# Packed attention with a convolved gate: half of batch 2's convolution on VectorE, and another order

## The chip, the cores and the metric

One core of one Trainium2 chip. The time is device microseconds of the whole kernel. It is the median of three runs: 284.44 us (283.52 to 285.25). The profile is of one more execution.

## The reference

For each of 8 batches, with S = 576 positions, 8 heads of 64 channels and 32 packed queries per head (everything in float32):

```python
p_packed = softmax(p @ k.T / 8) @ v              # 32 x 64 per head
x = softmax(q @ p_packed.T / 8) @ p_packed       # 576 x 64 per head, 576 x 512 over all heads
gate = sigmoid(sum(conv_w[k] * x_shifted(4 - k) for k in range(5)))   # causal, per channel
out = (gate * (x @ w_val)) @ w_out               # 512 x 512 weights
```

w_val, conv_w and w_out arrive as 64-bit floats; the kernel turns them into float32 itself.

## The kernel before, in words

Each batch is one chain of stages, and each stage is a Python generator that issues one or a few instructions per step. A written list, ORDER (line 52), names the stages by letter and batch (`x2` is one step of stage x for batch 2, `s3.2` two steps of stage s for batch 3); `run` (line 690) takes the steps in that order. InOrder (line 77) keeps every engine's instructions in the order in which they were issued, so ORDER is the program order of all engines. The stages, with the letters of the list:

- K, V, Q, P, L load k, v, q, p and the weights through SyncE's queue. `fetch` (line 188) makes each large load wait until the third load before it has landed (AT_ONCE = 3). v comes in two halves per batch; its tile vm has two buffers.
- W, C, O turn the words of the weights into float32 (ScalarE, VectorE, GpSimd); C also makes cwb, the taps spread over rows for the convolution on TensorE.
- k and q transpose on VectorE. a (line 375) is the first attention: scores on TensorE (tile s), maximum on VectorE (nb), exponential on ScalarE, which also accumulates the sums (sm); on VectorE the sums get 1e-9 added and are inverted; then the exponentials are turned (at, copied to a1t) and multiplied with v (pv), and ScalarE scales the product into ppd.
- p turns ppd. s (line 443) makes the second scores and exponentials. t (line 464) divides by their sums in two groups of heads, one behind the other: sums and reciprocals (rs) and a transpose (a, the tile a2) on VectorE, a product on GpSimd, and a split of a2 into a high and a low part (a2h, a2l).
- w multiplies the packed values with w_val (wp, split into wph and wpl).
- x (line 505) yields the gate's input. For a batch in WHOLE (0, 1 and 2) `convolved` (line 534) does the whole convolution on TensorE: GpSimd multiplies the packed values with the five taps (kx), and TensorE multiplies a2, shifted by 0 to 4 positions, with kx, in two halves of 288 positions; ScalarE takes tanh of each result (tile sig). For the other batches TensorE mixes once (tile x), ScalarE copies the result to xp, and stage g does the rest.
- g (line 576) is the convolution for the other batches: for each of four groups of 128 channels ScalarE multiplies with the first tap, VectorE adds the other four (scalar_tensor_tensor, each reading and writing sig), and ScalarE takes tanh. The four channel groups follow one another.
- v (line 597) multiplies a2 with the packed values (val), VectorE multiplies with the gate, ScalarE makes the high part gvh, GpSimd the low part gvl.
- o (line 643) multiplies with w_out (tile o), in chunks of 128 positions; the result goes through osb to memory. For the last batch the products of the first three channel groups are made ahead, and the ones with the fourth come last.

The tiles sig have four buffers, xp two (kx lies in one of them), PSUM's big tile three (lines 19 to 44).

Of the kernel before, what the change touches and what calls it, by code (L numbers as in the profile page):

```python
# [57 lines left out]
v0 t1 a3.2 P4 a3 w1 O0.2 Q2 O0 v0 w1.2 v0 q2 p2 O0.2 x1 a3 x1 O0 x1 a3.2 O0 t1 a3.2 x1 L0 t1 O0.2 V3 q2 a3 x1 P4 O0.2
v1 x1 O0 K4 v1 s2 O0 V4 a3 O0 k4 a3 O0 v1 K4 O0 k4 s2 K5 s2.2 v1 s2 o0 s2 o0 p3 k4 Q3 v1.3 t2 v1.2 K5 v1 Q3 v1.2 a4 q3
o0 t2 a4.2 s2 a4.2 w2 V4 o0 s2 v1 t2 o0 w2 k5 s2 p3 a4 x2 q3 o0 v1 o0 w2 t2 s3 t2 o0 P6 Q4 t2 a4 v1 t2 s3 P6 s3 t2  # L60
s3.2 t2 s3.2 k5 s3 o0.2 a4 s3 v1 x2.3 Q4 a4 K6 a4 k5 a4.2 x2 o0 q4 t2 a4 t3 x2 v2 q4 x2 t3 a5 t3 v2 t3 a4.2 o1 t3 o0
t3 k6 K6 a5 t3 V5 v2 a5.2 t3 x3 Q5 x3 a4 v2 a5 k6 x3.2 t3 k6 v2 o1 v2 p4 v2 x3.3 t3 V5 Q5 o1 g3 a5.2 g3 p4 a5 v2 g3 o1
g3 v2.2 o1 s4 g3 s4 v2 g3 o1 v2 g3 a5 q5 s4 V6 v2 K7 g3 a5 o1 s4 a5.2 s4 v2 s4 g3 a5 t4 o1 w3.2 g3 o1 s4.2 v2 a6 a5 g3
t4 v2 a6 q5 a6 w3 o1 t4 v3 s4 g3.2 a5 V6 a5 g3 o1 a6 t4 g3 t4 o1 a6 p5 t4 o1 g3 p5 v3 Q6 s5 o1 v3 a6 o1 g3.3 s5 t4 v3
s5.2 v3 Q7 g3 o2 v3 s5 t4 o2 v3 o2 s5 v3.2 g3.2 s5 t4 v3.2 g3 x4 g3 o2.2 x4 v3 x4 o2 x4 v3 x4 K7 t4 x4 k7 g4 o2 s5 t5
q6 v3.2 a6 x4 k7 a6 o2 g4 w4 t5 Q6 g4 w4 g4.2 a6 o2 g4.2 t5 w4 g4 V7 a6 t5 a6 s5 a6 t5 g4.2 t5 g4 v3 o2.2 v4 o2 a6 g4
o3 g4 v4 o3 v4 t5.2 v4 g4 v4 o3 g4 a6 v4.2 g4 v4.2 g4 q6 a6.2 g4.2 v4 g4.4 x5.2 p6 t5 x5 o3 p6 o3 s6 g4 v4 x5 o3.2 t5
s6 v4 s6 v4 o3 s6.2 o3 s6 x5.2 k7 g5 o3 x5 s6 v4 t6 g5 w5 o3 g5.2 w5 s6 o3 a7 g5 v4 g5 V7 w5 o3 a7 v5 g5.3 a7.2 s6 g5
v5 g5 o3 a7 t6 v5 v4 a7 v5 a7.2 q7 o4 o3 g5 a7 g5 t6 g5.2 a7.2 g5 a7 t6.2 g5 a7 o4 v5.2 Q7 a7.2 t6 a7 o4 g5 o4 t6 g5.2
v5.2 q7 p7 t6 p7 v5 o4 t6 v5 s7 g5 s7.3 o4 g5 v5 s7.2 o4 g5 x6.2 v5 x6.2 v5 x6 o4.2 t6 t7.2 g5 o4 v5 x6 g6 x6 v5 s7 g6  # L70
o4 g6 w6.2 g6.2 w6 g6 v5 t7 o5 g6 o5 g6 t7 o5 v6 s7 o4 g6.3 t7 o5 s7 t7.2 o5 g6.3 v6.3 g6.2 v6.2 o5.4 v6 g6.2 t7 v6 g6
v6.2 g6.3 o5.2 g6 x7 o5 v6.3 t7 x7 o5 g6 x7.2 v6.2 w7 t7 o5 x7 w7 v6 o6 w7 v7 x7 g7 o6 g7.6 o5 x7 v7 g7 o6.3 v7 g7.3
# [29 lines left out]
def packed_attention_gated_conv(  # L102
# [272 lines left out]
    def attn_pack(b):  # L375
# [6 lines left out]
        for g in range(G):  # L382
            nb = tile_of("nb1", [P, 1], F32, f"nb1_{b}_{g}")
            dve.tensor_reduce(nb, s1s[g], axis=AX.XY, op=ALU.max, negate=True)
            yield
            a1 = a1s[g] = tile_of("a1", [P, S], F32, f"a1_{b}_{g}")
            act.activation(
                a1.rearrange("a (c i m) -> a c i m", c=2, i=NP),
                in_turn(s1s[g]),
                AF.Exp,  # L390
                bias=nb,
                accum_out=sm[:, g : g + 1],
            )
# [68 lines left out]
            yield  # L462

    def weighted(b):
        rs = tile_of("rs2", [P, G, NBLK], F32, f"rs2_{b}")
        a2 = st["a2", b] = tile_of("a2", [P, G, S], F32, f"a2_{b}")
        ah = st["ah", b] = tile_of("a2h", [P, G, S], F32R, f"a2h_{b}")
        al = st["al", b] = tile_of("a2l", [P, G, S], F32R, f"a2l_{b}")
        for g in range(G):
            t3, r3 = st["t2", b][:, g], rs[:, g]  # L470
            dve.tensor_reduce(r3, t3, axis=AX.X, op=ALU.add)
            dve.reciprocal(r3, r3)
            yield
            t3 = t3[:, :, :NP]
            pool.tensor_tensor(
                t3, t3, r3.unsqueeze(2).broadcast_to([P, NBLK, NP]), op=ALU.mult
            )
            yield
            dve.transpose(a2[:, g], t3)
            yield  # L480
            act.copy(ah[:, g], a2[:, g])
            yield
            (pool if b in ON_POOL["al"] else dve).tensor_tensor(
                al[:, g], a2[:, g], ah[:, g].bitcast(F32), op=ALU.subtract
            )
            yield

# [46 lines left out]
    def convolved(b):  # L534

        kx = tile_of("xp", [P, 2, PAD + S], F32, f"kx_{b}")
        kx = kx.rearrange("a n m -> a (n m)")[:, : G * NT * D]
# [7 lines left out]
        yield
        sigs = []
        for c in range(NC):
            st["sig", b, c] = tile_of("sig", [P, S], F32, f"sig_{b}_{c}")
            sigs.append(st["sig", b, c])
        for half in range(2):  # L550
            a2 = st["a2", b]
            two = [big(f"x_{b}_{half}_{n}") for n in range(2)]
            for back in range(NT):
                skip = back if half == 0 else 0
                end = half * HS + HS - back
                for g in range(G):
                    for hl in range(4):
                        pe.matmul(
                            two[hl // 2][D * g : D * g + D, hl % 2, skip:HS],
                            kx[heads[hl], g, NT - 1 - back, :],  # L560
                            a2[heads[hl], g, end - HS + skip : end],
                            start=(back == 0),
                            stop=(back == NT - 1),
                        )
            yield
            for c in range(NC):
                act.activation(
                    sigs[c][:, half * HS : half * HS + HS],
                    two[c // 2][:, c % 2, :HS],
                    AF.Tanh,  # L570
                    scale=0.5,
                )
                if c % 2:
                    yield

    def gate(b):
        if b in WHOLE:
            return
        for c in range(NC):
            x = st["xp", b, c // 2][:, c % 2]  # L580
# [3 lines left out]
            for kk in range(1, NT):
                dve.scalar_tensor_tensor(
                    acc,
                    x[:, kk : kk + S],
                    cw[:, c, kk : kk + 1],
                    acc,
                    op0=ALU.mult,  # L590
                    op1=ALU.add,
                )
                yield
            act.activation(acc, acc, AF.Tanh, scale=0.5)
            yield
# [139 lines left out]
```

## Time and profile before

| | |
|---|---|
| median of three runs | 284.44 us |
| the profiled execution | 284.7 us |
| its span, first to last instruction | 282.9 us |
| TensorE matmul busy | 251.4 us (89%), 3603 instructions |
| TensorE weight loads busy | 186.8 us (66%) |
| VectorE busy | 237.2 us (84%), 313 instructions |
| ScalarE busy | 164.5 us (58%) |
| GpSimd busy | 129.4 us (46%) |
| granted TensorE clock, mean | 0.980 |

Busy shares are of the span. In the profile's lines PE is TensorE's matmul, PEld its weight load, DVE VectorE, ACT ScalarE, POOL GpSimd and SP SyncE's queue, which issues all transfers. Every instruction goes through the same helper, so all lines are L85, and groups are told apart by the tiles: out<-in. A matmul of 32-bit floats has two records. Matmuls of different parts of the array overlap, so that a group's busy time is more than the time for which it holds TensorE up; the chain of waits gives that time.

### The profile page before, as it was taken

How to read it: one execution, taken by the hardware profiler on the slowest of the kernel's cores; microseconds unless marked ns; L12 is line 12 of the kernel's file. 1: busy time of each engine (PE TensorE's matmuls, PEld its weight loads, DVE VectorE, ACT ScalarE, POOL GpSimd, SP SyncE). 2: the span in 40 equal slices, each digit the busy share in tenths (PEclk: the TensorE clock that was granted, in tenths of full speed). 3: DMA queues.
4: the chain of work that ended last, by engine and by line, in shares of the span. 5: the costliest groups of instructions: out<-in, count | busy, mean ns of one | idle time of the engine just before them, and what ended most of it. 6: DMA issues, size and time to landing. Idle time of an engine off the chain costs nothing.

```text
span 282.9 us, 8353 instructions
## 1 busy us (share of the span) xinstructions
PE 251.4 (89%) x3603; PEld 186.8 (66%) x3603; DVE 237.2 (84%) x313; ACT 164.5 (58%) x307; POOL 129.4 (46%) x118
## 2 busy tenths in 40 slices
PE   0366397999999999999999999999999899998984
PEld 0144254776786777786878687758876688687763
DVE  2978779799789997789999999999998989687720
ACT  6245564677934664864746765667747645743321
POOL 1633577667788572423466324243156423422220
PEclk9989879999999999999999999999999999999999
DMA  7999989599649758816552540116111112111014
GB/s 258 330 292 310 226 270 264 164 238 287 179 153 306 207 161 237 257 43 203 150 180 81 191 132 37 39 75 179 66 39 41 48 63 76 39 74 39 0 50 172
DMA packets 25858, 43.54 MB, mean 154 GB/s; under 512 B 5834, under 2 KB 11998, under 8 KB 25822
## 3 DMA queue, kind: packets, MB, share of 16 engines
q1 hardware_dynamic: 25822, 43.02, 49.5%
q8 instruction: 28, 0.46, 0.7%
q14 instruction: 8, 0.07, 0.1%
HBM read 33.57 MB, written 9.44 MB: 152 GB/s over the span
## 4 chain that ended last, share of the span: by engine, by line
PE 55%; DVE 23%; ACT 9%; DMA 5%; issue 3%; POOL 2%; SPq 2%; POOLq 1%; ACTq 0%; DVEq 0%
PE o L85 20%; DVE sig L85 16%; PE val L85 11%; PE s L85 7%; PE x L85 7%; PE pv L85 4%; DMA vm<-in_v_dram 3%; ACT sig L85 3%; PE at L85 3%; PE wp L85 2%; POOL t L85 2%; SPq L85 2%; DMA p<-in_p_dram 1%; ACT gvh L85 1%; ACT osb L85 1%
## 5 line engine op out<-in xcount | busy, mean ns | idle before, releaser
L85 DVE SCALAR_TENSOR_TENSOR sig<-xp,cw,sig 128x576 f32<-128x576 f32 x80 | 75.0, 937 | 6.1 <-ACT sig L85 4.6
L85 POOL TENSOR_TENSOR gvl<-sig,gvh 128x576 fp32r<-128x576 f32 x32 | 49.3, 1541 | 55.8 <-ACT gvh L85 55.8
L85 PE MATMUL o<-woh,gvh 128*128 128x512 f32 x144 | 59.1, 411 | 0.8 <-ACT osb L85 0.7
L85 PE MATMUL o<-woh,gvl 128*128 128x512 f32 x144 | 57.2, 398 | 1.2 <-POOL gvl L85 1.1
L85 PE MATMUL o<-wol,gvh 128*128 128x512 f32 x144 | 56.9, 395 | 0.0
L85 PE MATMUL val<-a2h,wph 128*128 128x288 f32 x128 | 39.1, 305 | 0.0
L85 PE MATMUL val<-a2h,wpl 128*128 128x288 f32 x128 | 38.0, 297 | 0.9 <-DVE wpl L85 0.9
L85 PE MATMUL val<-a2l,wph 128*128 128x288 f32 x128 | 37.6, 294 | 0.0
L85 POOL TENSOR_TENSOR t<-t,rs 128x576 f32<-128x576 f32 x16 | 20.0, 1252 | 34.7 <-DVE rs L85 34.7
L85 PEld LDWEIGHTS o<-woh,gvh 128*128 128x128 f32 x144 | 27.0, 188 | 12.6 <-ACT osb L85 2.7
L85 PEld LDWEIGHTS o<-woh,gvl 128*128 128x128 f32 x144 | 27.1, 188 | 8.8 <-POOL gvl L85 2.5
L85 ACT ACTIVATE osb<-o 128x512 f32<-128x512 f32 x34 | 20.4, 599 | 18.4 <-PE o L85 14.8
L85 ACT CAST gvh<-sig 128x576 fp32r<-128x576 f32 x32 | 21.5, 671 | 16.4 <-DVE sig L85 16.0
L85 PEld LDWEIGHTS o<-wol,gvh 128*128 128x128 f32 x144 | 27.1, 188 | 5.0
L85 DVE SCALAR_TENSOR_TENSOR sig<-sig,val 128x576 f32<-128x576 f32 x32 | 23.8, 743 | 7.8 <-ACT sig L85 3.6
L85 POOL TENSOR_TENSOR t<-t,mx 128x576 f32<-128x576 f32 x16 | 21.2, 1328 | 18.3 <-DVE mx L85 18.3
L85 PEld LDWEIGHTS val<-a2h,wph 128*128 128x128 f32 x128 | 24.0, 188 | 4.4 <-issue 1.8
L85 PE MATMUL s<-kT,pT 32*32 32x288 f32 x512 | 15.5, 461 | 11.7 <-DVE kT L85 11.7
L85 PEld LDWEIGHTS val<-a2h,wpl 128*128 128x128 f32 x128 | 24.0, 188 | 2.1 <-DVE wpl L85 1.2
L85 ACT ACTIVATE sig<-sig 128x576 f32<-128x576 f32 x20 | 13.7, 685 | 19.4 <-DVE sig L85 19.1
L85 PEld LDWEIGHTS val<-a2l,wph 128*128 128x128 f32 x128 | 24.1, 188 | 0.0
L85 PEld LDWEIGHTS pv<-vm,a1t 96*32 96x32 f32 x768 | 12.8, 117 | 15.1 <-ACT p L85 5.1
(81 smaller groups left out, 444.2 us busy)
## 6 DMA issues: line engine op xcount, KB each, us to landing
km<-in_k_dram SPq DMA_DIRECT2D x16, 576.0 KB, 5.3
vm<-in_v_dram SPq DMA_DIRECT2D x16, 576.0 KB, 6.1
qm<-in_q_dram SPq DMA_DIRECT2D x16, 576.0 KB, 6.1
out_dram<-osb SPq DMA_DIRECT2D x36, 256.0 KB, 2.0
wv_words<-in_moe_w_val_dram SPq DMA_DIRECT2D x4, 512.0 KB, 4.5
wo_words<-in_moe_w_out_dram SPq DMA_DIRECT2D x4, 512.0 KB, 5.6
p<-in_p_dram SPq DMA_DIRECT2D x16, 64.0 KB, 5.9
cw_words<-in_moe_conv_w_dram SPq DMA_DIRECT2D x1, 20.0 KB
```

The costliest lines, as they stand in the source:

```text
L85: made = getattr(self.engine, op)(*args, **kw)
```

## The change

Batch 2 leaves WHOLE and is alone in HALF: channel groups 0 and 1 are convolved on TensorE as before, groups 2 and 3 are mixed, copied to xp and convolved by stage g. Stage g now works on one channel group (`g10` is batch 2's third), so that the list can put the steps of several groups in any order. The second group of stage t is a stage of its own, u. The sums of the first attention go to a tile that is filled with 1e-9 at the start, and a reduction over two numbers takes the place of the scalar add. ORDER is another list from its second line on. Cut to its core:

```diff
-WHOLE = (0, 1, 2)
+WHOLE = (0, 1)
+
+HALF = (2,)
...
+    sums = const.tile([P, B, G, 2], F32, name="sums")
+    pool.memset(sums, 1e-9)
...
-                accum_out=sm[:, g : g + 1],
+                accum_out=sums[:, b, g, :1],
...
-        dve.tensor_scalar_add(sm, sm, 1e-9)
+        dve.tensor_reduce(sm, sums[:, b], axis=AX.X, op=ALU.add)
         dve.reciprocal(sm, sm)
...
+    def taps(b, kx, two, half, hls):
+
+        a2 = st["a2", b]
+        for back in range(NT):
+            skip = back if half == 0 else 0
+            end = half * HS + HS - back
+            for g in range(G):
+                for hl in hls:
+                    pe.matmul(
+                        two[hl // 2][D * g : D * g + D, hl % 2, skip:HS],
+                        kx[heads[hl], g, NT - 1 - back, :],
+                        a2[heads[hl], g, end - HS + skip : end],
+                        start=(back == 0),
+                        stop=(back == NT - 1),
+                    )
...
+    def half_and_half(b):
+
+        kx = factors(b)
+        pp = st["pp", b]
+        act.copy(pp, st["ppd", b][:, 2])
+        xp = st["xp", b, 1] = tile_of("xp", [P, 2, PAD + S], F32, f"xp_{b}_1")
+        pool.memset(xp[:, :, :PAD], 0.0)
+        yield
...
+            two = [big(f"x_{b}_{half}_{n}") for n in range(2)]
+            for g in range(G):
+                for hl in range(2, 4):
+                    pe.matmul(
+                        two[1][D * g : D * g + D, hl % 2, :HS],
+                        pp[heads[hl], g * D : g * D + D],
+                        a2[heads[hl], g, hc],
+                        start=True,
+                        stop=True,
+                    )
+            taps(b, kx, two, half, range(2))
+            yield
+            act.copy(xp[:, :, PAD + half * HS : PAD + half * HS + HS], two[1][:, :, :HS])
+            yield
...
-    def gate(b):
-        if b in WHOLE:
-            return
-        for c in range(NC):
+    def gate(n):
+        b, c = divmod(n, NC)
```

In the new list SyncE issues, after q of batch 0: v of batch 1 (first half), the first part of w_out, k of batch 2 (first half), p of batches 2 and 3, v of batch 1 (second half). Before, it was: the first part of w_out, k of batch 2 (first half), p, v of batch 1 (both halves). The steps around it and the last ones, old and new:

```diff
-V0 a0.2 W0 a1 W0 a0 W0 C0 a1 W0 a0 W0 Q0.2 a0 L0 p0 a1 K2 p0 q0.2 a1 P2 s0 a1 C0.2 s0 C0 O0 s0 O0 s0 V1 s0.2 a1 s0 O0
-a1 C0 t0 C0 | s0 C0 s0 a1 V1 t0 x0 P2 O0 t0.2 a1 t0.3 a1 k2 a1.2 w0 O0 t0 a1 w0 a1.2 x0 a1 t0 w0 O0 t0 O0 Q1 k2 K2 L0
...
-v7 o6 g7 v7 o6 g7 o6.2 g7 v7 g7 v7 g7.2 v7 g7 v7 o7 g7 v7 g7.4 o7 v7.2 g7 v7.2 o7 v7.2 o7.16 o6.3
+V0 a0.2 W0 C0 W0 C0 a1 a0 Q0 W0 Q0 V1 a0 L0 a1 a0 K2 a1 q0.2 C0 p0 P2 p0 a1 W0 s0 a1 W0 s0 O0.2 s0.2 C0 s0.3 a1.3 O0
+s0 t0 C0 s0 C0 | C0 u0 t0 a1.3 P2 a1 u0 x0 w0 O0 t0 V1 O0.2 a1 O0 a1.2 u0 w0 x0 t0 a1 u0 O0 x0 O0 p1 L0 k2 O0 k2 O0 x0
...
+v7 g30 o6 g30 g29 v7 g31 o6 v7.2 g29 v7 o6 v7.3 g30 o6 g30 v7 g31.2 v7 g31 v7 g31 v7 o7 v7 o6 o7 v7 o7.2 v7 o7.13 o6
+o7 o6 o7 o6
```

## Rows read from the trace of the kernel before

**Rows 1.** Windows of five stages: start:end, length, busy time per engine, PEclk, DMA.
```profile
0.00:40.00 40.00, 18.54 (x430) 11.43 (x434) 28.75 (x47) 20.45 (x40) 19.09 (x23) 0.87 0.94 278
40.00:100.00 60.00, 56.98 (x1184) 41.39 (x1174) 53.21 (x71) 37.56 (x79) 42.96 (x37) 1.00 0.78 230
100.00:130.00 30.00, 30.00 (x579) 22.60 (x578) 25.32 (x34) 19.09 (x41) 12.60 (x13) 1.00 0.60 178
130.00:230.00 100.00, 98.66 (x1166) 74.82 (x1165) 96.16 (x127) 65.11 (x114) 41.13 (x37) 1.00 0.31 98
230.00:270.00 40.00, 38.89 (x234) 31.02 (x233) 32.33 (x35) 19.72 (x32) 12.16 (x10) 1.00 0.12 47
```

**Rows 2.** Waits of PE from 39 us to the end: total, times, longest.
```profile
PE o L85 <- POOL gvl L85: 1.1, 2, 0.8
...
PE val L85 <- DVE wpl L85: 0.9, 1, 0.9
```

**Rows 3.** Chain that ended last, TensorE part: start, length, tile, matmuls.
```profile
105.35 2.61 PE x L85 x80
...
115.08 0.67 PE x L85 x16
```

**Rows 4.** Groups by line: count | busy, mean ns | idle before.
```profile
L85 DVE SCALAR_TENSOR_TENSOR sig<-xp,cw,sig 128x576 f32<-128x576 f32 x80 | 75.0, 937 | 6.1 <-ACT sig L85 4.6
...
L85 ACT ACTIVATE sig<-xp,cw 128x576 f32<-128x576 f32 x20 | 15.4, 769 | 0.3
...
L85 ACT ACTIVATE sig<-sig 128x576 f32<-128x576 f32 x20 | 13.7, 685 | 19.4 <-DVE sig L85 19.1
...
L85 ACT COPY xp<-x 128x576 f32<-128x576 f32 x20 | 12.2, 638 | 2.1 <-PE x L85 1.9
...
L85 ACT ACTIVATE sig<-x 128x288 f32<-128x288 f32 x24 | 8.0, 414 | 4.7 <-PE x L85 4.7
...
L85 ACT ACTIVATE ppd<-pv,sm 128x64 f32<-128x64 f32 (+1 forms) x32 | 9.6, 340 | 10.3 <-PE pv L85 8.1 <-issue 1.1 <-ACT sig L85 1.0
```

**Rows 5.** Tile sig: ns min/median/max of the convolution taps.
```profile
L85 DVE SCALAR_TENSOR_TENSOR sig<-xp,cw,sig x80: 719/818/2064, 120.9 to 267.1; 128x576 f32<-128x576 f32 x80
```

**Rows 6.** Tile sm: ns min/median/max of the two short VectorE operations.
```profile
L85 DVE TENSOR_SCALAR sm<-sm x8: 158/554/1572, 17.8 to 197.1; 128x2 f32<-128x2 f32 x8
...
L85 DVE RECIPROCAL sm<-sm x8: 165/165/167, 18.7 to 197.3; 128x2 f32<-128x2 f32 x8
```

**Rows 7.** Timeline of VectorE, two stretches: start, length, operation.
```profile
149.25 0.82 DVE L85 SCALAR_TENSOR_TENSOR sig<-xp,cw,sig 128x576 f32<-128x576 f32 x1
...
149.99 0.75 DVE L85 TENSOR_REDUCE mx<-t 128x18 f32<-128x576 f32 x1
...
157.82 4.43 DVE L85 SCALAR_TENSOR_TENSOR sig<-xp,cw,sig 128x576 f32<-128x576 f32 x4
...
237.74 3.38 DVE L85 SCALAR_TENSOR_TENSOR sig<-xp,cw,sig 128x576 f32<-128x576 f32 x4
```

**Rows 8.** Timeline of GpSimd beside the four taps at 157.82.
```profile
158.43 1.50 POOL L85 TENSOR_TENSOR gvl<-sig,gvh 128x576 fp32r<-128x576 f32 x1 [2.11 <-ACT gvh L85]
```

**Rows 9.** Timeline of all engines, 22 to 42 us.
```profile
22.11 0.35 SPq L85 DMA_DIRECT2D wo_words<-in_moe_w_out_dram  x1
...
25.86 1.41 SPq L85 DMA_DIRECT2D vm<-in_v_dram  x2
...
31.60 0.68 ACT L85 ACTIVATE t<-t 128x576 f32<-128x576 f32 x1 [1.89 <-POOL t L85]
...
34.41 0.78 ACT L85 COPY a1t<-at 96x768 f32<-96x768 f32 x1
...
35.90 1.51 PE L85 MATMUL pv<-vm,a1t 96*32 96x64 f32 x48 [4.92 <-DMA vm<-in_v_dram]
...
40.56 1.78 PE L85 MATMUL x<-a,kx 32*64 32x288 f32 x36
```

**Rows 10.** Tile vm up to 50 us: loads of v, issue to landing.
```profile
DMA to landing us min/median/max: 6.1/7.6/10.2
```

More of the change, by code (lines that the diff above doesn't have):

```diff
@@ L58 @@
[L58 to L72, printed above, removed]
@@ new lines @@
+a3.2 w1 a2.2 a3 v0 p2 w1 p2 O0 w1 u1 V3 q2 t1 v0 O0.2 x1.2 a3 x1 Q2 a3 P4 q2 a3 P4 O0 a3 O0 V3 x1 a3.2 L0 O0.3 u1 x1
+Q3 O0 v1 O0 x1 s2 O0.2 v1 K4 k4 v1 O0 s2 k4 v1 O0 v1.2 s2 v1 Q3 v1 s2 v1 o0 K4 a3 o0 k4 s2 a3 K5 s2 v1 a4 K5 s2 w2
+o0.2 s2 q3 v1 a4 p3 a4 s2 v1 V4 t2 a4 v1 a4 u2 t2 q3 w2 t2 v1 o0 a4 u2 t2 k5 P6 o0 v1 o0 x2 a4 p3 w2 s3 o0 u2.2 a4 k5
+v1 s3 u2 o0 s3 a4 s3 x2 P6 a4 x2 s3.3 o0 s3 k5 t2 x2.2 t3 s3 Q4 x2.2 v2 u3 g10 q4 a4 g11 u3.2 V4 v2 a5 V5 a4 g10 g11
+o0 o1 a5 a4 g10 a5.2 t3 a5 g11 u3 t3 g11 g10 g11 a4 v2 K6 a4 g10 K6 Q4 x3.2 v2 o1 v2 x3 a5 a4 p4.2 v2 k6 o1 q4 x3 v2
@@ new lines @@
+g10 v2 o0 v2.2 x3.2 o1 g12 k6 Q5 g13 g12 a5 x3 a5 g13 s4 o1 v2 g12 a5 g13 o1 t3 g11 s4 k6 V5 q5 u3 a5 v2 Q5 t3 a5.2 o1
+a5 s4 g12 g14 s4 v2 o1.2 s4 v2 s4 o1 g13 a5 s4 v2 a6 s4 o1 t4 w3 o1 q5 a5 a6 o1 a5 t4 w3 s4 a6.2 p5 a6 v2 t4 w3 t4 g12
+p5 v3 s5 g14 o1 g12 K7 g15 t4 u4 o2 V6 g14 s5 o2 v3 K7 g14 g15 u4 v3 g13 o2 g14 v3 g13 u4 s5 g14 v3 o2 g15 v3 s5 o1 v3
+o2 s5 v3.2 s5 g15 v3 s5 Q6 g15 u4 x4 V6 x4 v3 o2 v3 o2 x4 s5 g15 x4.2 v3 o2 u4 a6 o2 x4 w4 t5 x4 a6 g16 q6 s5 v3 g16
+v3 g17 w4 u5 a6 o2 g18 g16 g17 w4 g16 Q6 a6 o2 a6 g17 g18 a6.3 g17 t5 v4 g16 g17 v3 g19 g18 o3 g16 v4 a6 o3 V7 a6 v4
@@ new lines @@
+g19 u5 v4 g18 o3 v4 t5 g17 a6 v4.2 u5 g18 v4 t5 v4 g18 q6 g19 v4 o2 p6 g19 Q7 g19 t5 k7 p6 x5.3 o3.2 v4 s6 o3 v4 s6 x5
+o3 s6 x5 g19 s6 x5 o3 g21 s6.2 Q7 v4 k7 u5 k7 s6 g21 v4 x5 g21 o3 g22 o3.2 g22 v4 a7 w5 g20 u5 a7 w5 a7.3 g20 o3 w5 V7
+g20 a7 o3 g20 v4 a7 s6 v5 o3 a7.3 g20.2 g22 a7.3 o4 t6 v5 s6 a7 g22 g23 g21 a7.2 o4 q7 g22 g21 v5 u6 v5 o4 v5 u6 p7
+g21 v5 g22 o3 p7 t6 o4 v5 g23 v5 q7 v5 o4 u6 v5 t6 u6 s7 o4.2 g23 s7.2 v5.2 s7 g23 o4 s7.2 t6 g23.2 s7 x6 o4 t6 v5
+x6.2 o4 x6 v5 s7.2 w6 u6 o4 x6 t7 v5 w6 u7 x6 g25 w6 g24 g25 g24 v5 o5 g24 g25 v6 o5 x6 g25 g26 o4 g27 o5 g26 g24.2 o5
@@ L464, in weighted, with weighted_second, weighted_group @@
     def weighted(b):
[L465 to L486, printed above, removed]
+        st["rs", b] = tile_of("rs2", [P, G, NBLK], F32, f"rs2_{b}")
+        st["a2", b] = tile_of("a2", [P, G, S], F32, f"a2_{b}")
+        st["ah", b] = tile_of("a2h", [P, G, S], F32R, f"a2h_{b}")
+        st["al", b] = tile_of("a2l", [P, G, S], F32R, f"a2l_{b}")
+        yield from weighted_group(b, 0)
+    def weighted_second(b):
+        yield from weighted_group(b, 1)
+    def weighted_group(b, g):
+        rs, a2, ah, al = (st[nm, b] for nm in ("rs", "a2", "ah", "al"))
+        t3, r3 = st["t2", b][:, g], rs[:, g]
+        dve.tensor_reduce(r3, t3, axis=AX.X, op=ALU.add)
+        dve.reciprocal(r3, r3)
+        yield
+        t3 = t3[:, :, :NP]
+        pool.tensor_tensor(
+            t3, t3, r3.unsqueeze(2).broadcast_to([P, NBLK, NP]), op=ALU.mult
+        )
+        yield
+        dve.transpose(a2[:, g], t3)
+        yield
+        act.copy(ah[:, g], a2[:, g])
+        yield
+        (pool if b in ON_POOL["al"] else dve).tensor_tensor(
+            al[:, g], a2[:, g], ah[:, g].bitcast(F32), op=ALU.subtract
+        )
+        yield
     def packed_values(b):
@@ L508, in mixed @@
             yield from convolved(b)
+            return
+        if b in HALF:
+            yield from half_and_half(b)
             return
@@ L532, in mixed, with factors @@
                 yield
-    def convolved(b):
+    def factors(b):
         kx = tile_of("xp", [P, 2, PAD + S], F32, f"kx_{b}")
-        kx = kx.rearrange("a n m -> a (n m)")[:, : G * NT * D]
-        kx = kx.rearrange("a (g k d) -> a g k d", g=G, k=NT)
+        kx = kx.rearrange("a n m -> a (n m)")
+        st["pp", b] = kx[:, G * NT * D : G * (NT + 1) * D]
+        kx = kx[:, : G * NT * D].rearrange("a (g k d) -> a g k d", g=G, k=NT)
         pool.tensor_tensor(
@@ L544, in convolved @@
         )
+        return kx
+    def taps(b, kx, two, half, hls):
[11 more added lines that the diff above has]
+                        stop=(back == NT - 1),
+                    )
+    def half_and_half(b):
[4 more added lines that the diff above has]
+        pool.memset(xp[:, :, :PAD], 0.0)
+        yield
+        sigs = []
+        for half in range(2):
+            hc = slice(half * HS, half * HS + HS)
+            a2 = st["a2", b]
+            two = [big(f"x_{b}_{half}_{n}") for n in range(2)]
[7 more added lines that the diff above has]
+                        stop=True,
+                    )
+            taps(b, kx, two, half, range(2))
+            yield
+            act.copy(xp[:, :, PAD + half * HS : PAD + half * HS + HS], two[1][:, :, :HS])
+            yield
+            for c in range(2):
+                if half == 0:
+                    st["sig", b, c] = tile_of("sig", [P, S], F32, f"sig_{b}_{c}")
+                act.activation(
+                    st["sig", b, c][:, half * HS : half * HS + HS],
+                    two[0][:, c % 2, :HS],
+                    AF.Tanh,
+                    scale=0.5,
+                )
+            yield
+    def convolved(b):
+        kx = factors(b)
         yield
@@ L550, in convolved @@
         for half in range(2):
-            a2 = st["a2", b]
             two = [big(f"x_{b}_{half}_{n}") for n in range(2)]
[L553 to L564, printed above, removed]
+            taps(b, kx, two, half, range(4))
             yield
@@ L574, in convolved @@
                     yield
-    def gate(b):
-        if b in WHOLE:
-            return
-        for c in range(NC):
-            x = st["xp", b, c // 2][:, c % 2]
-            acc = st["sig", b, c] = tile_of("sig", [P, S], F32, f"sig_{b}_{c}")
-            act.mul(acc, x[:, :S], cw[:, c, 0:1])
-            yield
[L584 to L595, printed above, removed]
+    def gate(n):
+        b, c = divmod(n, NC)
+        x = st["xp", b, c // 2][:, c % 2]
+        acc = st["sig", b, c] = tile_of("sig", [P, S], F32, f"sig_{b}_{c}")
+        act.mul(acc, x[:, :S], cw[:, c, 0:1])
+        yield
+        for kk in range(1, NT):
+            dve.scalar_tensor_tensor(
+                acc,
+                x[:, kk : kk + S],
+                cw[:, c, kk : kk + 1],
+                acc,
+                op0=ALU.mult,
+                op1=ALU.add,
+            )
+            yield
+        act.activation(acc, acc, AF.Tanh, scale=0.5)
+        yield
     def value(b):
```

8 lines of the change are left out of this document (5 added, 3 removed).

## The prediction

> **What bounds the kernel now.** I read the busy times by stage first. In the first 40 us TensorE is busy for 18.5 us only; from 40 us to 270 us it idles 3.0, 0.0, 1.3 and 1.1 us per stage, at a granted clock of 1.00 [rows 1]. So after the start the kernel is as long as TensorE's own work. VectorE is the next bound: it idles 6.8 us in 40 to 100, 4.7 us in 100 to 130, but only 3.8 us in the hundred microseconds from 130 to 230, and 7.7 us from 230 to 270 [rows 1]. ScalarE and GpSimd have a third of each stage or more free. The waits of TensorE after 39 us are short; the ones with a producer that this change touches are 1.1 us for the low part of the gated values and 0.9 us for the low part of the packed values [rows 2]. The large loss is at the start: the first product with v of batch 1 begins at 35.90 after 4.92 us of idle, and its load was only issued at 25.86 [rows 9].
>
> So a microsecond counts in full where it is taken from TensorE after 40 us, or from what starts its dense stretch. On VectorE it counts only where the stage's idle time is used up.
>
> **TensorE's convolution of batch 2.** One half of a fully convolved batch is 80 matmul records and 2.61 us; one half of a batch that only mixes is 16 records and 0.67 us [rows 3]. With two of four channel groups each, a half costs 1.31 + 0.34 = 1.65 us, so the two halves together save 2 x 0.96 = 1.9 us. This is in the stage where TensorE never idles: minus 1.9.
>
> **VectorE.** Two channel groups get four taps each: 8 more taps. A tap is 937 ns in the mean [rows 4], 818 ns in the median, up to 2064 ns [rows 5]; 8 x 937 = plus 7.5 us. Two things go the other way. The scalar add on two numbers takes 158 ns at best, 554 in the median and 1572 at worst, while the reciprocal behind it always takes 165 [rows 6]. The long ones are waits, not arithmetic. A reduction stays at 0.75 us beside GpSimd's work (149.99) [rows 7], so I price the new reduction like the reciprocal: 8 x (554 - 165) = minus 3.1 (bounds: 0 if it waits as the add did, minus 3.1). Then the order: four taps of one channel group in a row take 3.38 us, which is (3.38 - 0.82) / 3 = 0.85 us from start to start, while a tap followed by unrelated work gives way after 149.99 - 149.25 = 0.74 us [rows 7]. In the old order 39 of 80 taps directly follow the tap that they need, in the new one 14 of 88 (counted in the two lists): 25 x 0.11 = minus 2.8 (bounds: 0 and minus 2.8). Net on VectorE: 7.5 - 3.1 - 2.8 = plus 1.6 us. The new taps fall due while TensorE does batch 2's values and batch 5's attention, about 100 to 130 us, where VectorE idles 4.7 us [rows 1], and the savings lie mostly behind that. I cost it at 0; the cover is that idle time. If it is gone, the price is 1.6 us, and up to 7.5 if neither saving comes.
>
> **What slows a tap.** Four taps that should take 3.38 us took 4.43 while GpSimd computed a low part from 158.43 on for 1.50 us [rows 7, 8]: one meeting costs 1.05 us. From mean and median, meetings cost 80 x (937 - 818) = 9.5 us in all, some nine of them [rows 4, 5]. The Trainium skill speaks against the change here (GPSIMD Engine Reference, section Key points): GpSimd shares its SBUF interfaces with VectorE, and contends with instructions in a two-port mode or with two SBUF inputs. Each added tap has two SBUF inputs, and the trace agrees with the rule; that every added tap stands open to such a meeting is the slower rival below. A second rule disagrees with the rows: a tap alone takes about 0.82 us [rows 5, 7]. The Trainium skill (Vector Engine (DVE) Microarchitecture Reference, section Points that are easy to get wrong) says that a scalar-tensor-tensor with two SBUF sources wider than bf16 runs at half rate; at the 0.96 GHz of VectorE: DVE Perf Modes (Specifications) an estimate for 576 elements is 1.2 us, 9.6 us for the eight, and by that the net on VectorE would be 3.7. The measurement decides.
>
> **ScalarE and GpSimd.** Of batch 2's eight half tanhs four stay. The four that go are 4 x 414 = 1.7 us; two copies (638), two first products (769), two full tanhs (685) and a small copy (like 340) come, 4.5 us [rows 4]: plus 2.8 us, hidden by ScalarE's idle 10.9 us of 100 to 130 [rows 1]. GpSimd gains two short clears, hidden likewise. A wait is added: batch 3's clears on GpSimd need the buffer that batch 2's last taps read, and behind them in GpSimd's queue stand the first low parts of batch 2's values and batch 4's scores. In the new list the last tap stands just before, so I cost it at 0; if VectorE is late there, its lateness is passed on, as in the slower rival.
>
> **The start.** The load of v's first half for batch 1 now stands ahead of a weight load, a load of k, and eight small loads of p on SyncE's queue; these all come later by one load's turn. It cannot go before the third load ahead of it has landed, which is when the weight load was issued: 22.11 instead of 25.86 [rows 9]. With 6.1 to 10.2 us to landing [rows 10] it arrives at 28.2 to 32.3, not 35.8. What is late next is ScalarE: the copy that this product also needs ran at 34.41, behind two exponentials and two copies; in the new order it stands right behind the first exponential, which ended at 31.60 + 0.68 = 32.28 [rows 9]. So the product can start at 32.28 + 0.78 = 33.1, 2.8 us sooner. The first convolution (40.56 [rows 9]) needs more: the second half of v, issued at about 28 and landed at 34 to 38, and the two transposes on VectorE, between which weight steps stand that can wait for GpSimd. I take minus 2.0 for TensorE's dense stretch, between 0 (something else there is as late) and the whole wait, minus 4.9.
>
> **The other moves.** The second group's softmax weights get a stream of their own, and gates are made one channel group at a time. The work is the same; the gain is in the waits. At the end the last two low parts kept TensorE waiting 1.1 us [rows 2], behind gates that ran as one chain of four taps; now two to three gates are under way at once, so I take minus 1.1 (bounds: 0, and minus 2.0 with the 0.9 us of [rows 2]; the other way, VectorE's idle 3.8 us between 130 and 230 shows how little lateness the order can hide).
>
> **Sum.** 1.9 + 2.0 + 1.1 = 5.0 us off. The profiled execution took 284.7 us (span 282.9 and 1.8 around it): 279.7. The median of the runs is 0.26 lower: 279.4 us, which I round to 279.5.
>
> **Rivals.** (a) Slower: the meetings of taps and GpSimd double. Interleaved gates put taps into more of GpSimd's work, which is busy 41 of 100 us from 130 to 230 [rows 1]. Nine more meetings are plus 9.5 us, with the net 1.6 that is 11.1 us; the idle 4.7 us of 100 to 130 and the 2.0 us from the start take part of it, and VectorE ends 11.1 - 4.7 - 2.0 = 4.4 us later: 284.4 + 4.4 = 288.8. It decides from a mean tap of about 1.0 us upwards (6.7 - 1.6 = 5.1 us over 88 taps is 58 ns more than today's 937). Against it: the same number of GpSimd operations meets hardly more taps. Chance 0.13. (b) Hardly any change: the start does not move, since the first convolution waits for the GpSimd products and transposes rather than for v, or because the load that is meant to be sooner lands with the other loads in the same crowd; and VectorE's 1.6 us come out of TensorE's 1.9. That gives about 284. For it: in the first 40 us TensorE's granted clock is 0.87 in the mean, so some of it ran at 1.2 GHz instead of 2.4, and VectorE is busy 28.8 of the 40 [rows 1]. Chance 0.15. (c) Better: the whole 4.9 us and the 2.0 us of waits go, besides the 1.9: 284.4 - 8.8 = 275.6. Chance 0.12. The forecast has 0.60, with its own range from 277 to 282.5.
>
> **The numbers.** About half a percent, 1.4 us, is what a measurement of this kernel can tell from no change. Faster by more than that: the forecast, (c) and a little of (b): 0.74. Within it: 0.13. Slower: (a) and what is left: 0.13. The range leaves out half of (c) and most of (a): 276.0 to 285.5.
>
> **What would show it.** Right: batch 2's matmuls of the mixing tile shrink by 1.9 us in sum; the short step on the sums stays under 0.25 us; the mean tap stays under 0.95 us; the first product with v of batch 1 starts near 33 us and the first convolution near 38.5; TensorE idles no more than 6 us after that. Wrong: VectorE's gate or transposes release TensorE in stages between 100 and 230 us where it did not wait before, the mean tap rises over 1.0 us, or the first convolution still starts at 40.

## The result, and the profile after

The changed kernel takes 281.78 us (median of 19 runs, 278.04 to 284.07), the kernel before 283.98 us (19 runs beside them, 282.93 to 285.71). By these medians 2.2 us are off (0.992), where 5.0 had been forecast. The ratio, 0.9889 with a 95% interval of 0.9865 to 0.9912, counts only the eleven of the 19 runs in the fast state, those within 1.5% of the fastest one, and so makes the gain look about a microsecond larger. A second set of seven runs, below, gives 0.9913. The profile shown here is that of a second execution of the changed kernel (280.32 us, span 278.5 us); the first took 283.76 us, near the top of the 19, because its start was 2.7 us later and the stretch from there to the values of batch 2 0.7 us longer. From the values of batch 2 on the two agree within 0.1 us. (The helper that issues every instruction is line 90 there, and line 85 to 94 in the other kernels.)

The windows of the five stages, changed kernel; they answer to [rows 1]:

```profile
0.00:40.00 40.00, 21.02 (x474) 12.40 (x474) 29.74 (x48) 20.64 (x41) 18.46 (x23) 0.91 0.97 285
40.00:100.00 60.00, 57.30 (x1208) 41.48 (x1205) 51.33 (x72) 39.81 (x83) 45.57 (x40) 1.00 0.72 209
100.00:130.00 30.00, 30.00 (x451) 22.41 (x444) 26.78 (x38) 20.70 (x40) 9.61 (x12) 1.00 0.64 177
130.00:230.00 100.00, 100.00 (x1167) 76.40 (x1166) 95.51 (x131) 64.39 (x113) 43.84 (x38) 1.00 0.35 111
230.00:270.00 40.00, 38.84 (x235) 31.48 (x235) 29.93 (x35) 20.08 (x32) 12.08 (x10) 1.00 0.12 45
```

TensorE is still what the kernel waits for, now without a gap from 100 to 230 us. In 100 to 130 it has 128 matmul records fewer than before (451 against 579) and is busy all the same; but only 64 of them are the convolution's (48 records a half instead of 80), the rest is work that now falls on the other side of the window's edges. What the missing records were worth is told by the chain that ended last. The two halves of batch 2's convolution, changed kernel (start, length, tile, matmuls; against [rows 3]):

```profile
98.16 2.77 PE x L90 x48
...
103.89 2.61 PE x L90 x48
```

48 records take as long as 80 did: the records went and the time did not. On VectorE, the groups by line and the short steps (against [rows 4, 5, 6]):

```profile
L90 DVE SCALAR_TENSOR_TENSOR sig<-xp,cw,sig 128x576 f32<-128x576 f32 x88 | 75.2, 886 | 0.9 <-ACT sig L90 0.4
...
L90 DVE TENSOR_REDUCE sm<-sums x8: 143/149/156, 17.7 to 193.6; 128x2 f32<-128x4 f32 x8
```

Eighty-eight taps take as much time as eighty did (75.2 against 75.0 us), and the short step on the sums never takes longer than 156 ns any more.

So where do the 2.2 us come from? I cut each trace at three events of TensorE: its first convolution (batch 0), its first value product of batch 2, its first value product of batch 7. The lengths in us:

| | start to first convolution | to values of batch 2 | to values of batch 7 | to the end |
|---|---|---|---|---|
| before | 40.6 | 67.3 | 139.1 | 35.9 |
| changed (profile shown) | 39.5 | 66.9 | 138.5 | 33.6 |
| changed (first profile) | 42.2 | 67.6 | 138.6 | 33.6 |

From the values of batch 2 on the changed kernel is 2.8 us shorter in both profiles (172.2 and 172.1 against 175.0 us). Most of it, 2.3 us, is in the last column. Before, the chain of waits through the last stage was not TensorE's (kernel before, chain that ended last):

```profile
245.52 0.79 ACT sig L85
246.33 0.83 DVE sig L85
247.19 0.83 DVE sig L85
...
249.75 0.69 ACT sig L85
250.46 1.50 DVE sig L85 x2
...
267.99 0.70 ACT sig L85
268.70 0.77 DVE sig L85
269.49 0.68 ACT gvh L85
...
270.28 1.47 POOLq L730
...
271.79 0.51 PE o L85
```

ScalarE's first product, four taps, tanh, gate, and the same again for each of the last four channel groups, each step waiting for the one before, on its own engine or on the other; TensorE waits for the low part of the gated values three times. (POOLq L730 is GpSimd's queue with the low part gvl.) In the changed kernel the same view has TensorE alone:

```profile
249.43 1.58 PE val L90 x12
251.01 2.75 PE o L90 x12
253.76 3.17 PE val L90 x24
256.93 11.00 PE o L90 x48
...
267.96 0.61 ACT osb L90
```

48 output matmuls run without a break, and the only waits left are for the copies of the result (osb). VectorE's timeline shows why (changed kernel; the four taps at 246.33 above are the same stretch before):

```profile
244.36 6.30 DVE L90 SCALAR_TENSOR_TENSOR sig<-xp,cw,sig 128x576 f32<-128x576 f32 x8 [0.19 <-ACT sig L90]
250.57 0.75 DVE L90 SCALAR_TENSOR_TENSOR sig<-sig,val 128x576 f32<-128x576 f32 x1
251.24 4.37 DVE L90 SCALAR_TENSOR_TENSOR sig<-xp,cw,sig 128x576 f32<-128x576 f32 x4
```

Eight taps of several channel groups in a row, 6.30 / 8 = 0.79 us each instead of 0.85, and a tanh of one group runs under the taps of another. The last gate is done at 264.2 us instead of 269.5.

### The profile page after: what moved, and what is told of

Read it like the earlier page. It is cut to its first block, busy times and chain, and to the rows that moved or that the text cites. A ratio compares the mean times of both kernels' runs of the same rounds, so it can differ in the third digit from the quotient of the medians.

```text
span 282.0 us, 8248 instructions
## 1 busy us (share of the span) xinstructions
PE 252.8 (90%) x3539; PEld 187.8 (67%) x3539; DVE 235.1 (83%) x321; ACT 167.4 (59%) x310; POOL 129.6 (46%) x120
## 4 chain that ended last, share of the span: by engine, by line
PE 81%; DVE 10%; issue 3%; ACT 2%; DMA 2%; SPq 1%; POOL 0%; ACTq 0%; DVEq 0%
PE o L90 36%; PE val L90 17%; PE s L90 9%; PE x L90 7%; PE pv L90 4%; PE at L90 4%; PE wp L90 3%; DMA p<-in_p_dram 2%; DVE sig L90 1%; DVE kT L90 1%; DVE mx L90 1%; DVE t L90 1%; PE ppTt L90 1%; DVE a L90 1%; SPq L90 1%
## 5 line engine op out<-in xcount | busy, mean ns | idle before, releaser
L90 DVE SCALAR_TENSOR_TENSOR sig<-xp,cw,sig 128x576 f32<-128x576 f32 x88 | 75.2, 887 | 0.9 <-ACT sig L90 0.4
L90 PE MATMUL o<-woh,gvh 128*128 128x512 f32 x144 | 58.5, 406 | 1.2 <-ACT osb L90 1.2
L90 ACT ACTIVATE osb<-o 128x512 f32<-128x512 f32 x34 | 20.4, 599 | 27.1 <-PE o L90 22.7
L90 PEld LDWEIGHTS o<-woh,gvl 128*128 128x128 f32 x144 | 27.1, 188 | 5.9
L90 PEld LDWEIGHTS o<-wol,gvh 128*128 128x128 f32 x144 | 27.1, 188 | 4.8
L90 POOL TENSOR_TENSOR t<-t,mx 128x576 f32<-128x576 f32 x16 | 20.6, 1289 | 17.5 <-DVE mx L90 17.2
L90 PE MATMUL s<-kT,pT 32*32 32x288 f32 x512 | 16.7, 479 | 11.9 <-DVE kT L90 11.6
L90 POOL TENSOR_TENSOR t<-t,rs 128x576 f32<-128x576 f32 x16 | 20.7, 1305 | 7.5 <-DVE rs L90 6.0
L90 DVE STREAM_TRANSPOSE qT<-qm 128x1152 f32<-128x1152 f32 x16 | 21.5, 1348 | 2.1 <-DMA qm<-in_q_dram 2.1
L90 DVE STREAM_TRANSPOSE kT<-km 128x1152 f32<-128x1152 f32 x16 | 21.5, 1352 | 0.6 <-DMA km<-in_k_dram 0.6
```

The source lines that it names most:

```text
L90: made = getattr(self.engine, op)(*args, **kw)
```

## The experiments

Ratios are to the kernel before, in runs on the same chip.

**The changed kernel again**, as the measure for the others.

> The changed kernel once more, for another profile and beside the next three. Theory 1 (the start is a loss: the sooner load of v crowds q of batch 0, and the first convolution starts later than before): the second half of q lands after 27 us again, the first convolution of batch 0 starts at 41 us or later, and the rest of the kernel is some 3.5 us shorter. Theory 2 (the late start was one execution's chance): the first convolution starts between 38 and 40 us. Both: about 0.989 of the kernel before.

Measured: 281.24 us, 0.9913 (0.9871 to 0.9954). The second half of q lands at 26.2 us and the first convolution starts at 39.5, as the second theory had it; but the later profiles of this start scatter up to 42.5 us.

**The end alone.** Two kernels exchange the list from the first step of batch 7's gates on (`g7` in the old list, `g28` in the new one). The old kernel with the new end, for which stage g of batch 7 works on one channel group as in the change (this version of the stage has the letter h in the list):

```diff
-... w7 v7 x7 g7 o6 g7.6 o5 x7 v7 g7 o6.3 v7 g7.3 v7 o6 g7 v7 o6 g7 ...
+... w7 v7 x7 h28.3 h29 o5 h28 o6 h29 x7 h28 h29 o6 h30 h29 h30 h31 o6 h28 ...
```

> The kernel before with the end of the new list alone: from the first gate of batch 7 on, the steps stand as in the changed kernel (gates one channel group at a time, two or three under way). If the gain of the change lies at the end: 2 to 2.5 us faster, ratio 0.991 to 0.993; from TensorE's first value product of batch 7 to the end 33.6 us instead of 35.9. If it lies in the other parts: 0.997 to 1.003.

Measured: 281.73 us, 0.9913 (0.9879 to 0.9946). And the changed kernel with the old end, the same edit the other way:

> The changed kernel with the old list's end, from the first gate of batch 7 on (the four channel groups one after the other). If the gain lies at the end: about 2.3 us slower than the changed kernel, ratio 0.997 to 1.000, and 35.9 us from the first value product of batch 7 to the end. If not: as the changed kernel, 0.990.

Measured: 285.64 us, 1.0046 (1.0013 to 1.0079). So, within the intervals, the end alone brings what the change brings, and without it nothing is left. The traces tell more finely: from the values of batch 2 on it is 175.0 us before, 173.1 with the new end alone and 172.2 in the changed kernel, so that about two of the 2.8 us are the end's; what the other 0.9 go with is told under the sums. The chain of the old kernel with the new end is TensorE's again:

```profile
258.82 11.20 PE o L87 x48
...
270.04 0.60 ACT osb L87
```

and that of the changed kernel with the old end is the old chain:

```profile
267.75 0.69 ACT sig L90
268.46 0.77 DVE sig L90
269.25 0.68 ACT gvh L90
...
270.04 1.44 POOLq L792
...
271.53 0.51 PE o L90
```

The last stretch is 33.9 us in the first and 37.6 in the second. (The 35.9 that was expected was missed: of the 37.6, some 1.5 are clock. Behind two waits of 0.8 and 0.7 us TensorE's granted clock is 0.5, which is 1.2 GHz, from 273.1 to 276.5 us, and nine output matmuls there take 3.90 us instead of 2.37.)

**Batch 2 whole on TensorE**, in the new order:

```diff
-WHOLE = (0, 1)
+WHOLE = (0, 1, 2)
-HALF = (2,)
+HALF = ()
```

with `g10` and `g11` taken out of the list.

> The changed kernel with batch 2 convolved on TensorE alone again, steps g10 and g11 left out of the list. If the 1.9 us of TensorE come off the end in full: 1.9 us slower than the changed kernel, ratio 0.995 to 0.997 of the kernel before. If VectorE's eight more taps (7 us) cost as much as TensorE gains: no difference from the changed kernel (0.989). If VectorE is the bound: faster than the changed kernel.

Measured: 281.89 us, 0.9921 (0.989 to 0.9951), the same as the changed kernel. Its chain:

```profile
97.97 2.69 PE x L90 x80
100.66 2.96 PE o L90 x12
103.63 2.61 PE x L90 x80
```

80 records or 48, the halves take 2.6 to 2.8 us. VectorE is busy 228.6 us instead of 234.4, and TensorE has no use for those 5.8 us: from the first convolution to the values of batch 2 it takes 67.0 us instead of 66.9, and 172.2 from there to the end, as in the changed kernel.

**Batch 2 whole on VectorE**, to see what TensorE's share is worth. All four groups are mixed only; two gates of the four run in a burst right behind the mixing, since there are four buffers sig, and the copy of the packed values is kept in cwb's space:

```diff
-HALF = (2,)
+HALF = ()
+MIXED_ONLY = (2,)
...
-... x2 ...
+... x2 g8 g9 g8 g9 g8 g9 g8 g9 g8 g9 g8 g9 ...
```

> The changed kernel with all four channel groups of batch 2 convolved by VectorE, the two added ones in a burst behind batch 2's mixing (their packed values are held in a tile of their own). TensorE's mixing of batch 2 should take 2 x 0.67 = 1.3 us instead of 5.4, which saves 4 us; VectorE gets 8 more taps, some 6.6 us, where it idles 3.2 us of 30. If TensorE's saving counts: 0.975 to 0.985. If VectorE passes its lateness on: 0.990 to 1.005.

Measured: 288.71 us, 1.0121 (1.0065 to 1.0176), slower than both theories. The chain shows both sides of it:

```profile
99.80 0.77 PE x L92 x16
100.56 2.96 PE o L92 x12
103.53 0.72 PE x L92 x16
...
105.46 0.68 ACT sig L92
...
106.16 5.92 DVE sig L92 x8
```

With no taps left on TensorE the two halves take 1.5 us instead of 5.4, so 3.9 us can be had, but not by halves: from the first convolution to the values of batch 2 it takes 63.0 us instead of 66.9. From there to the values of batch 7 it takes 149.4 instead of 138.5. TensorE stands for 8.0 us behind the burst of eight taps, as the waits of PE show:

```profile
PE at L92 <- DVE sig L92: 8.0, 1, 8.0
```

In that wait (107.8 to 115.9 us) its granted clock falls to 0.5, which is 1.2 GHz, from 111.6 to 121.8 us. Whether four groups dealt out over 100 to 130 us would win was not tried.

**The load of v.** The changed kernel with the first half of v of batch 1 back behind w_out, k and p:

```diff
-... Q0 W0 Q0 V1 a0 L0 a1 a0 K2 a1 q0.2 C0 p0 P2 p0 ...
+... Q0 W0 Q0 a0 L0 a1 a0 K2 a1 q0.2 C0 p0 P2 V1 p0 ...
```

> The changed kernel with the load of v's first half for batch 1 back behind w_out, k and p. Theory 1: q lands sooner by some 2 us, and the kernel is faster than the changed one by 1 to 3 us: 277 to 280 us, 0.98 of the kernel before. Theory 2 (the forecast's start term, minus 2.0 for the sooner load): slower than the changed one by 1 to 3 us, about 0.995.

Measured: 280.42 us, 0.9889 (0.9845 to 0.9933), beside 0.9913 for the changed kernel: it is no slower, and not faster by more than the intervals hide. And the kernel before with that load ahead of w_out:

```diff
-... W0 Q0.2 a0 L0 p0 ... s0 V1 s0.2 ...
+... W0 Q0.2 V1 a0 L0 p0 ... s0 s0.2 ...
```

> The kernel before with nothing but that load moved ahead of w_out's first part. Theory 1: slower by 0 to 2 us, ratio 1.000 to 1.007. Theory 2: faster by about 2 us, ratio 0.993; at least 0.7 us are lost to ScalarE's queue, where the copy that the product needs ends only at 35.2.

Measured: 285.05 us, 1.0039 (1.0013 to 1.0065). The sooner load brings nothing in one order and costs 1 us in the other, inside the first theory's range. In the changed kernel the first product with v has another wait (timeline, changed kernel):

```profile
31.93 0.69 ACT L90 ACTIVATE t<-t 128x576 f32<-128x576 f32 x1 [0.94 <-POOL t L90]
32.52 0.78 ACT L90 COPY a1t<-at 96x768 f32<-96x768 f32 x1
33.41 0.68 ACT L90 ACTIVATE t<-t 128x576 f32<-128x576 f32 x1
34.00 0.68 ACT L90 COPY cwb<-spread 128x640 f32<-128x640 f32 x1
34.56 0.12 DVE L90 COPY cw<-cwps 128x20 f32<-128x20 f32 x1
34.78 1.51 PE L90 MATMUL pv<-vm,a1t 96*32 96x64 f32 x48 [3.27 <-ACT cwb L90]
39.52 1.87 PE L90 MATMUL x<-a,kx 32*64 32x288 f32 x37
```

v was issued at 21.98 and there by 28.7 us, and the copy a1t was done at 33.3. The product began when ScalarE's cwb and VectorE's cw had ended, both at 34.68, and the profile names cwb. But the kernel's text has the product read neither: it is written to the one PSUM buffer that the turned taps (cwps) hold until VectorE's copy cw has read them. In the new list cw stands behind the sums (rs) of batch 0's second attention. So the wait is, by the kernel's text, for VectorE and that buffer; the two copies end together in every profile in which the product starts behind them, so that no run separates them. In the old kernel with the load sooner it is q that pays (timeline, kernel before with v sooner):

```profile
22.42 0.33 SPq L85 DMA_DIRECT2D vm<-in_v_dram  x1
...
27.98 1.38 DVE L85 STREAM_TRANSPOSE qT<-qm 128x1152 f32<-128x1152 f32 x1 [1.77 <-DMA qm<-in_q_dram]
```

VectorE waits 1.77 us for the second half of q of batch 0, which lands at 28.0 us instead of 25.6, and the first convolution comes at 43.3 us instead of 40.6.

**ScalarE's order at the start.** The changed kernel with the copy a1t of batch 1 behind the second exponential and cwb:

```diff
-... s0.3 a1.3 O0 s0 t0 C0 s0 C0 | C0 u0 t0 ...
+... s0.3 a1.2 O0 s0 t0 C0 s0 C0 | C0 a1 u0 t0 ...
```

> The changed kernel with one step of ScalarE moved back: the copy that the first product of batch 1 with v needs stands again behind the second exponential of batch 0 and the copy of the convolution's taps. If ScalarE's order is what brings the start forward: that product and the first convolution start 1 to 2 us later, ratio 0.994 to 0.997. If the start hangs on the loads alone: no change, 0.990.

Measured: 281.83 us, 0.9918 (0.989 to 0.9946): not to be told from the changed kernel. The product starts 9.3 us behind the landing of q's second half, where the others with the new start have 8.6 to 10.0. The first convolution starts at 40.7 us, in the middle of what all the profiles show: 39.1 to 42.5 us over ten with the new start (mean 41.0; two of the ten have v late), 40.6 to 42.5 over three with the old one (mean 41.6). It goes with the landing of q's second half, and that scatters from run to run: 25.8 to 28.0 us in nine profiles with v's load ahead of w_out (mean 27.1), 25.6 to 26.4 in five without (mean 26.0). Counted from that landing the first convolution comes after 14.2 us in the mean of the ten, and after 15.5 in the mean of four with the old start. So by these means, of few profiles, the sooner load of v loses 1.1 us on q, and the rest of the new start gains 1.3.

**The sums.** The kernel before with the tile sums and the reduction, and the changed kernel with the old scalar add:

```diff
-        dve.tensor_scalar_add(sm, sm, 1e-9)
+        dve.tensor_reduce(sm, sums[:, b], axis=AX.X, op=ALU.add)
```

> The kernel before with nothing but the reduction over two numbers for the scalar add. The step should take 0.15 to 0.2 us each instead of 0.55 in the median. If VectorE's time counts on the path, up to 3 us faster (0.990); if it is covered by VectorE's idle time, no change (0.997 to 1.003). My forecast needs the first only in part: I expect 0.997.

Measured: 284.79 us, 1.0028 (0.9993 to 1.0063): no change, and not the 0.997 that was expected.

> The changed kernel with the scalar add on the two sums again instead of the reduction. VectorE's busy time rises by about 3 us. If VectorE is close to the bound in the new order: 1 to 3 us slower (0.993 to 1.000). If not: no change (0.989).

Measured: 282.26 us, 0.9935 (0.9907 to 0.9963). The step itself behaves as forecast, 148 ns in the median in the first and 538 (up to 1394) in the second, but it is worth little: 0.5 to 1.0 us in the new order, against the two sets of runs of the changed kernel (the intervals overlap), and nothing that could be told in the old one. The traces do tell it apart in the new order: from the values of batch 2 to the end it takes 173.3 us with the scalar add, and 172.1 to 172.4 in six profiles with the tile sums (the changed kernel twice, with v late, with batch 2 whole on TensorE, with the copy late, and with both doubtful parts undone, below). Even that may not come from VectorE; see the last section.

**The gates in line.** The changed kernel with every batch's gate steps at the same places of the list, but dealt out one channel group after the other; for batch 7:

```diff
-... g28.3 o6 g29 o5 g28 v7 o6 g29 x7 g28 g29 o6 g30 ...
+... g28.3 o6 g28 o5 g28 v7 o6 g28 x7 g29 g29 o6 g29 ...
```

> The changed kernel with the steps of the gates dealt out one channel group after the other, at the same places of the list. If the interleaving pays as forecast (0.11 us for each tap that no longer stands right behind the one it needs, and VectorE no longer waiting for ScalarE between groups): 2 to 4 us slower than the changed kernel, ratio 0.996 to 1.003. If those waits were covered by TensorE's work: within 1 us of the changed kernel.

Measured: 308.91 us, 1.0876 (1.0824 to 1.0928), far outside both theories. The mean tap is 935 ns, as before, but VectorE idles while TensorE waits:

```profile
L94 DVE SCALAR_TENSOR_TENSOR sig<-xp,cw,sig 128x576 f32<-128x576 f32 x88 | 82.3, 935 | 22.1 <-ACT sig L94 20.5
```

Before a tap 22.1 us are lost, 20.5 of them to ScalarE's step of the same channel group; 0.9 in the changed kernel. The places of the new list fit interleaved gates only, so this tells the price of the hand-offs more than what the order gained.

**Both doubtful parts undone**: batch 2 whole on TensorE and v late, the two edits above together.

> The changed kernel with two of its parts undone at once: batch 2 whole on TensorE (VectorE's share of it gone) and V's first half back behind w_out, k and p. What is left of the change is the order of the gates at the end, the convolution per 128 channels, ScalarE's order at the start and the reduction. Theory (the gain lies in the order of the end, and neither the split nor the sooner load carries any of it): 0.988 to 0.993 of the kernel before, 280.5 to 282.0 us, with the stretch from TensorE's first value product of batch 7 to the end at 33.6 us (35.9 before). Rival one (the split gives TensorE some 1.9 us and the sooner load some 2.0 at the start, as forecast, and one alone covers for the other): 1.000 or above, 284 to 285 us. Rival two (VectorE's eight taps and the load sooner cost something each, hidden in the scatter): 0.984 or below, under 279.5 us.

Measured: 280.46 us, 0.9872 (0.9834 to 0.991). The last stretch is 33.6 us, as expected, and the time is a hair under the theory's range (280.5). The chain is the same:

```profile
260.21 11.00 PE o L90 x48
```

With neither the split nor the sooner load the gain is all there, so rival one is out; rival two wanted under 279.5 us, and none of the six runs is there (279.69 to 283.59). That this version beats the changed kernel (281.78 us) can't be said, since the intervals overlap.

## Why the prediction was right or wrong

The sign and the range held (281.78 us in 276.0 to 285.5), the time is 2.3 us above the forecast of 279.5, and the gain is 2.2 us by the medians instead of 5.0. That it fell so well into the range is partly luck: of the three terms of the sum, 1.9 brought nothing and 2.0 nothing that stands out of the scatter, 1.1 became 2.0, and about 1 us came with a part of the change that I had costed as VectorE's time alone.

**TensorE's convolution of batch 2, minus 1.9: this is the step that failed.** I shared a half's 2.61 us out by channel groups, half the groups for half the time. The runs show 2.77 and 2.61 us for 48 records, 2.69 and 2.61 for 80, 0.77 and 0.72 for 16. The four channel groups lie on four strips of 32 rows of the array (times two halves of 64 columns) and run side by side. In the traces the 80 records start in ten waves of eight, 0.24 to 0.29 us from wave to wave and 7 ns from record to record within one; the 48 start in two waves of eight and eight of four, at the same distance; the 16 in two waves of eight. So two strips emptied leave two with ten records each, as long as before. (The row of the first convolution had the 32 rows already [rows 9].) The Trainium skill (TensorE: Matmul & The Clock Gate, Part 3: Packing small matmuls — row/col tiling, The mechanism) says that matmuls in different row groups overlap, so that the number of tiles adds next to nothing to the span. The trace agrees, with 48 records in 2.61 us; by that rule the term would have been next to 0, and I didn't weigh it.

**VectorE, plus 1.6, costed at 0: right in the time, wrong in the sum.** Forecast were 7.5 - 3.1 - 2.8. Eighty-eight taps took 0.2 us more than eighty, and VectorE's busy time fell from 237.2 to 234.4 us. The mean tap fell from 937 to 886 ns with nearly the same median (818 and 811), so most of that are fewer meetings with GpSimd: 88 x (886 - 811) = 6.6 us in all against 9.5. In the traces eight taps take over 1 us, against twelve before, and lose 6.9 us over the median instead of 10.3. The saving by the order came out as forecast: in the changed kernel a tap starts 0.73 us (median of 35) behind one that it doesn't need and 0.85 behind one that it needs, the taps overlap, and the 78.0 us of their single times fill only 75.2. So the eight taps more cost 8 x 0.81 = 6.5, the order gave 2.8 and the meetings 3.4; the last had no term in my sum. The reduction gave its 3 us (8 x (591 - 149) = 3.5, by means). Batch 2 whole on TensorE shows that VectorE's share was covered: 5.8 us less on VectorE, no difference in time. Rival (a), meetings that double, is out: it wanted a mean tap of 1.0 us.

**The start, minus 2.0: the cause was wrong, and of the gain hardly any is left.** The step named the load of v. Undone, it changes nothing that could be told (0.9889, beside 0.9913), and done alone it costs 1 us (1.0039), because q lands later. The load itself came as forecast (28.7 us), but "what is late next is ScalarE" was not the whole of it: its copy a1t was done at 33.3, and the product started at 34.8. By the kernel's text it waited for a PSUM buffer, which VectorE's copy cw frees at the end of a chain that begins with q's second half; the working had no term for that buffer. The first convolution is 0.6 us sooner in the mean of the profiles, in a scatter of 3.4.

**The end, minus 1.1: the right mechanism, too small.** Measured in the last stretch: 2.3 us. I took the 1.1 us from the table of waits [rows 2], which counts the idle time of two waits for the low part. In the trace of before TensorE starts its next output matmul 1.16, 0.73 and 0.48 us after the one before it at three places (260.39, 265.80 and 271.31 us), where 0.23 is usual: 0.92 + 0.50 + 0.25 = 1.7 us lost; the third is not among the table's two. The first two times the matmul behind the wait also took 0.34 us to the next one, 0.11 more than usual, 0.2 in all. That makes 1.9 of the 2.0 us that the old kernel with the new end gained; the rest, 0.3, is the faster output matmul below. The better sign was the chain of waits at the end: it ran through VectorE and ScalarE from 245 to 270 us, so that TensorE had to stop there, and only the distances of its matmuls told for how long.

**What the sum had no term for.** With the tile sums each output matmul follows the one before about 4 ns sooner (last section). From the values of batch 2 on, the changed kernel is 0.9 us shorter than the old one with the new end (172.2 against 173.1), and 1.1 us shorter than itself with the scalar add (173.3).

**Rivals (b) and (c).** (b), no change, named the right failures (the start does not move, the split is worth nothing) but had no gain at the end. (c), both waits and the whole 4.9 us of the start, is out.

**What would have shown it** worked: "batch 2's matmuls shrink by 1.9 us in sum" failed, "the short step under 0.25 us" and "the mean tap under 0.95" held. The signs for the start failed too: the product near 33 us (34.8), the first convolution near 38.5 (39.1 to 42.5, and "still at 40" was a sign of being wrong). And TensorE idles 7.7 us after the first convolution in the profile shown, less than the 10.1 before, but more than the 6 allowed.

## What to carry to other kernels

Before a part of a packed matmul is taken away, ask which strips of the array it empties: in these runs time went only where the longest strip got shorter. A chain of short steps that goes to and fro between two engines is broken by running two such chains side by side, and it is worth it where that chain sets the end, here in the last 35 of 284 us only. Where a load is pulled forward, look at what it pushes back, and whether the product that needs it also waits for a buffer. And a wait is better priced by the distance of the instructions around it, in the chain that ended last, than by the idle time in a table of waits.

## What the runs showed of the hardware

- **A matmul's rate went with a small tile.** From one output matmul (128x512) to the next it takes 233 ns (232.8 to 233.2 in five stretches from 50 us on) in the four kernels without the tile sums, 229 ns (229.0 to 230.1) in the nine with it, whatever their order. The 48 output matmuls in a row show it: 11.20 us in the old kernel with the new end and in the changed kernel with the scalar add (below), 11.00 in the changed kernel.

```profile
259.88 11.20 PE o L90 x48
```

  Over 3 x 144 output matmuls that is 432 x 3.8 ns = 1.6 us if all of it counts; the changed kernel with the scalar add, which has no such tile, takes 1.1 us longer from the first value product of batch 2 to the end (173.3 against 172.2). The rate changed both ways, when the edit was made in the old kernel and when it was undone in the new one. The tile holds 128 bytes of each partition and moves all that is laid out behind it. The step that reads it last ran at 194 us, and the rate differs at 260 us too, so I take the place of the other tiles for the cause; that is not shown, since no run separates the tile from the reduction.
- **Taps that don't depend on each other follow faster**, 0.73 us from start to start (median of 35 pairs in the changed kernel) instead of 0.85.
- **A scalar add on 128x2 numbers waits for the end of the GpSimd instruction that runs when it starts; a reduction to the same tile does not.** In the four kernels with the scalar add, all 19 adds that took over 200 ns (464 to 1572) end 21 to 27 ns after a GpSimd instruction; the other 13 took 127 to 164. Over all profiles 28 reductions ran wholly inside a GpSimd instruction, and they took 113 to 158 ns. Two of the adds (timeline, kernel before; 17.61 + 1.04 = 18.65 and 17.77 + 0.91 = 18.68):

```profile
17.61 1.04 POOL L85 TENSOR_TENSOR wv_words<-wv_words 128x512 f32<-128x512 f32 x1 [4.73 <-ACT a L85]
17.77 0.91 DVE L85 TENSOR_SCALAR sm<-sm 128x2 f32<-128x2 f32 x1 [0.17 <-ACT a L85]
...
30.41 1.16 POOL L85 TENSOR_TENSOR t<-t,mx 128x576 f32<-128x576 f32 x1 [4.13 <-DVE mx L85]
30.94 0.64 DVE L85 TENSOR_SCALAR sm<-sm 128x2 f32<-128x2 f32 x1
```
